# Splitting the last two output blocks of a recurrent attention step into column halves

## The chip, the core and the metric

The kernel runs on one core of one Trainium2 chip. The core has five engines that work side by side and meet through semaphores: TensorE (matrix products, PE in the profile; its weight loads are listed as PEld), VectorE (DVE), ScalarE (ACT), GpSimd (POOL) and SyncE (SP), which here only issues transfers. Matrix products are summed in PSUM, a small memory of eight banks; VectorE and ScalarE copy results out of it. Everything else lies in SBUF, and weights that do not fit there come from the chip's main memory again in every step, by DMA. The metric is the device time of one execution in microseconds (us). Before the change it is 1872.4 us, the median of three runs (1871.83 to 1874.24).

## What is computed

The reference has two parts that share nothing but the output array. Part B is a long convolution with a state-space kernel; the change does not touch it. Part A is attention over 64 segments of 32 rows, one after the other, with a memory of 8 rows that each segment passes on to the next:

```
for s in range(n_seg):                      # 64 segments
    xs = x[:, s * seg_len:(s + 1) * seg_len, :]
    h = concatenate([mem, xs], axis=1)      # 8 + 32 rows, 1024 wide
    q, k, v = h @ Wq, h @ Wk, h @ Wv        # 32 heads of 128
    p = softmax(where(mask, q k^T * scale, -1e9))
    o = (p v) @ Wo                          # back to 1024 columns
    mem = o[:, :8, :]                       # the state of the next segment
    outs.append(o[:, 8:, :])
```

So the output projection of one segment must be finished, at least for the memory rows, before the key, query and value projections of the next can begin.

## The kernel before

Part B runs first, together with all work of part A that does not depend on the memory: the projections of the last 8 rows of each segment are made ahead for all segments and stored in main memory (PKd holds their keys and queries, VXd their values and the other 24 rows of the input, transposed). Then comes a loop over 64 steps, one per segment (`part_a`, from line 408). After the loop a last stage makes the output rows that were left over.

In a step the stationary operand of a projection is `hT`, the transposed input: 32 columns (24 rows of the segment and the 8 memory rows) for each of eight blocks of 128 features, the "key blocks" kc 0 to 7. Since 32 columns fill a quarter of TensorE's array, four matmuls of 512 columns run side by side in four column strips (`quads`, line 409). A block of weights is 128 x 2048. Most blocks stay in SBUF all the time; 13 per step are streamed from main memory through five slots (`stage`, line 340, issued by SyncE; a slot's next load waits until its last reader is done). Three blocks live elsewhere: key block 7 of the first key projection, half of query block 7, and half of output block 15. They are kept in PSUM as raw words, and in every step VectorE copies them into a work area in SBUF just ahead of their use (`fetch`, line 364, through `words`, line 337). Key block 7 comes in five pieces, K7a to K7d and one in a small tile `S_`; the half of output block 15 comes in three, Oa, Ob and again `S_`.

The work area (`arena`) is one tile in which many short-lived tiles share places, by the table `AT` of line 37: "pk", the keys and queries made ahead for the next step, lies at place 0.

The order of the work is the order in which the program is written: each engine runs its own instructions strictly in that order (`manual_schedule`), and waits are derived from which places are read and written. A step has this order: key projection of the first 16 heads (k0), query projection (q0), then the same for the second 16 heads, values, and between them transposes, scores, softmax (VectorE and ScalarE) and the products with the values. Then the output projection `oproj` (line 522) adds 16 blocks into one PSUM tile `pp[:, 1, :]`: four strips of 32 rows, each strip 256 of the 1024 output columns, so a block has eight matmuls of 256 columns. Blocks 0 to 7 take the first 16 heads, and the order of the others is 8, 10, 12, 14, 9, 11, 13, 15; block 13 is streamed, block 15 is the half-fetched one.

What follows is the boundary between two steps (lines 624 to 643). The sums are copied to SBUF as `osb` in two halves of 128 columns, the first by VectorE and the second by ScalarE (line 627); TensorE makes a small product for the left-over rows (`pl`, line 629), transposes both halves (line 633), and VectorE copies the eight memory rows of each transposed half into `hT` (line 635). The first half holds the even key blocks and the second the odd ones; k0 takes the blocks in the order 0, 2, 4, 6, 1, 3, 5, 7. Behind the second of these copies VectorE fetches key block 7 (line 637). ScalarE issues the load of the next "pk" (line 640) and the store of the step's results (line 643) on its own queue; GpSimd later copies parts of "pk" beside the keys (line 430), and the scores (line 441) need them.

Of the kernel before, what the change touches and what calls it, by code (L numbers as in the profile page):

```python
# [10 lines left out]
BF16 = mybir.dt.bfloat16  # L11
F32 = mybir.dt.float32
I32 = mybir.dt.int32
I16 = mybir.dt.int16
ALU = mybir.AluOpType
# [21 lines left out]
AT = {"K7a": 3072, "K7b": 1024, "K7c": 2048, "K7d": 4192, "ob": 4960, "pk": 0, "vx": 3392, "Q7a": 2048, "Q7b": 3072,  # L37
# [3 lines left out]


def weight_blocks(Wq, Wk, Wv, Wo):
# [221 lines left out]
def load_resident(tc, pool, src, key, W_res, eng=None, t_=None):  # L265
    if t_ is None:
        t_ = pool.tile([128, 2048], BF16, name="W_%s" % "_".join(str(i) for i in key))
    (eng or tc.nc.sync).dma_start(out=t_[:].rearrange("e (h d) -> e h d", h=2) if key[0] == "o" else t_[:], in_=src(key))
    W_res[key] = t_


def part_a(ctx, tc, x, src, WD, HE, seg_len, out_a, ahead, W_res, rest, places, first):
    nc = tc.nc
    S, Dm = x.shape
    M = 8
    SL = seg_len
    E = 128
    KC = Dm // 128
    NS = S // SL
    assert SL == 32 and M == 8 and Dm == 1024 and HE == 4096  # L280
    XM = 24
# [5 lines left out]
    ident, mask, BD, BDx, BDL, hT = ahead.consts  # L287
# [14 lines left out]
    def unit(key):  # L302
        if key in rest:

            rest.remove(key)
            load_resident(tc, wres, src, key, W_res, None, outs.pop(0) if outs else places.pop(0)() if places else None)
        if key in W_res:
            return W_res[key]
        if key in KEPT:
            return ahead_of.pop(key) + halves.get(key, [])  # L310
        between.pop(key, lambda: None)()
        if key in first:
            return first.pop(key)
        t_ = stage(key, WD[key][:])
        if key[0] == "v":
            for k_ in rest[0:3 if key[1] == 0 else 1]:
                rest.remove(k_)
                load_resident(tc, wres, src, k_, W_res, None, outs.pop(0) if outs else places.pop(0)() if places else None)
        return t_
# [3 lines left out]
    ps = ctx_l.enter_context(tc.tile_pool(name="a_ps", bufs=1, space=PSUM))  # L323
# [4 lines left out]
    def at(name, *dims):  # L328

        n = int(np.prod(dims))  # L330
        t_ = arena[:, AT[name] // 2:AT[name] // 2 + n]
        if len(dims) == 1:
            return t_
        names = "abc"[:len(dims)]
        return t_.rearrange("p (%s) -> p %s" % (" ".join(names), " ".join(names)), **dict(zip(names, dims)))
# [28 lines left out]
    def fetch(key):  # L364

        ahead_of[key] = []
        for name, lo, n in KEPT[key]:
            t_ = at(name, n) if name else S_[:, 0:n]
            words(t_, kept[key][lo // 1024][:, lo % 1024 // 2:(lo % 1024 + n) // 2])
            ahead_of[key].append((lo, n, t_))  # L370

    def columns(w, lo, n):

        if not isinstance(w, list):
            return [(0, w[:, lo:lo + n])]
        return [(max(lo, l_) - lo, t_[:, max(lo, l_) - l_:min(lo + n, l_ + n_) - l_]) for l_, n_, t_ in w if l_ < lo + n and lo < l_ + n_]
# [31 lines left out]
    for s in range(NS):  # L408
        def quads(m, t, kcs, a=None):
            if a is None:  # L410
                a = ps.tile([128, 512], F32, name="acc", tag=BANK[m, t])
            for kc in kcs:
                w = unit((m, t, kc))
                for g in range(4):
                    for o_, rhs in columns(w, 512 * g, 512):
                        nc.tensor.matmul(a[32 * g:32 * g + 32, o_:o_ + rhs.shape[1]], lhsT=hT[:, kc, :], rhs=rhs,  # L416
                                         start=(kc == 0), stop=(kc == KC - 1), tile_position=(0, 32 * g), skip_group_check=True)
            return a

        def evac(a, name):  # L420
            q = at(name, 512)
            nc.scalar.copy(out=q, in_=a[:])  # L422
            return q
# [95 lines left out]

            pv(pl, t, V, L[:, 0].rearrange("p (a b) k -> p a (b k)", a=4), [L[:, 1].rearrange("p a k -> p (a k)")])  # L520

        def oproj(po, us, oT):
            for u in us:
                w = unit(("o", u))
                for hh in range(2):
                    h = 2 * u + hh
                    for qt in range(4):
                        for o_, rhs in columns(w, 1024 * hh + 256 * qt, 256):
                            nc.tensor.matmul(po[32 * qt:32 * qt + 32, o_:o_ + rhs.shape[1]], lhsT=oT[:, h % 4, (h % 16) // 4, :], rhs=rhs,  # L529
                                             start=False, stop=(h == 31), tile_position=(0, 32 * qt), skip_group_check=True)  # L530

        a = quads("k", 0, (0, 2, 4, 6, 1, 3, 5, 7))
        k0 = evac(a, "k0")
        if s == 0:
            for key in (("q", 0, 7), ("k", 0, 7), ("o", 15)):
                load_kept(key)
        a = quads("q", 0, range(0, 6))
# [5 lines left out]
        a = quads("k", 1, range(0, 3))  # L543
# [16 lines left out]
        a = quads("q", 1, range(KC))  # L560
# [3 lines left out]
        a = quads("v", 0, range(0, 4))  # L564
# [34 lines left out]
        a = quads("v", 1, range(0, 5))  # L599
        vl = vx[:, 0:256].rearrange("p (t e) -> p t e", t=2)  # L600
        pv0 = pv_x(0, V0, pb0, lb0)
        pp = ps.tile([128, 2, 256], F32, name="pp", tag="b3")
# [5 lines left out]
        lb1 = at("lb1", 512)  # L608
# [9 lines left out]
        o1 = evac_o(pv1, "o1", 2)  # L618
        lt1 = turn(weigh(sc1, 1, "ln1"), "lt1")
        oproj(pp[:, 1, :], range(5, 8), o0)  # L620
        L1 = left_blocks(lt1, 0, "L1")
        fetch(("o", 15))
        oproj(pp[:, 1, :], (8, 10, 12, 14, 9, 11, 13, 15), o1)
        ob = at("ob", 2, 256)
        osb = ob[:, 0, :]
        for j in range(2):
            (nc.scalar.copy if j else nc.vector.tensor_copy)(out=osb[:, 128 * j:128 * j + 128], in_=pp[:, 1, 128 * j:128 * j + 128])  # L627
        pl = ps.tile([128, 4, 32], F32, name="pl", tag="b2")
        pv_l(pl[:], 1, V1, L1)
        if s + 1 < NS:  # L630
            pt_o = [ps.tile([128, 4, SL], BF16, name="tro", tag=tag) for tag in ("b0", "b1")]
            for j in range(2):
                nc.tensor.transpose(out=pt_o[j][:].rearrange("p a b -> p (a b)"), in_=osb[:, 128 * j:128 * j + 128], identity=ident[:])
            for j in range(2):
                nc.vector.tensor_copy(out=hT[:, :, XM:SL].rearrange("p (q j) r -> p j q r", j=2)[:, j], in_=pt_o[j][:, :, XM:SL])
        if s + 1 < NS:
            fetch(("k", 0, 7))
        nc.scalar.copy(out=ob[:, 1, 0:128], in_=pp[:, 0, 0:128])
        if s + 1 < NS:
            pk = load_pk(s + 1)  # L640
        nc.scalar.copy(out=ob[:, 1, 128:256], in_=pl[:].rearrange("p a k -> p (a k)"))
        if s + 1 < NS:
            stores(s, ob)

    order = sorted(range(16), key=lambda u: ("o", u) not in W_res)
# [18 lines left out]
    for b in range(4):  # L664
        pe = [ps_k.tile([128, 512], F32, name="pe", tag="keep%d" % (2 * (b % 2) + n)) for n in range(2)]
        for u in order:
            for hh in range(2):
                h = 2 * u + hh
                hi = 16 * (h // 16) + 4 * (h % 4) + (h % 16) // 4
                for n in range(2):  # L670
                    nc.tensor.matmul(pe[n][:], lhsT=left[2 * b + hi // 16][:, 128 * (hi % 16):128 * (hi % 16) + 128],  # L671
                                     rhs=wo[u][:, 1024 * hh + 512 * n:1024 * hh + 512 * n + 512], start=(u == order[0] and hh == 0),
                                     stop=(u == order[-1] and hh == 1))
# [1129 lines left out]
```

## Time and profile before

| | |
|---|---|
| median of three runs | 1872.4 us (1871.83 to 1874.24) |
| profiled execution, its own time | 1879.37 us |
| span of its profile | 1877.7 us |
| granted TensorE clock, mean | 0.98 |
| TensorE busy | 1766.8 us (94%) |
| VectorE busy | 1344.5 us (72%) |
| ScalarE busy | 925.1 us (49%) |
| moved by DMA | 627.78 MB, mean 334 GB/s |

The profile is one execution, recorded by hardware. Its rows name the line of the kernel, the engine, the operation, what is written and read (`out<-in`), the shapes and, behind "x", how many instructions are merged in the row. In a timeline the first two numbers are the start and the duration in us from the start of the span; the bracket at the end is the idle time of the engine before, and who ended it. A row of waits gives the waiting engine, line and tile, then whom it waited for, the total in us, how often, and the longest. In a row by stretch each engine's busy time and instruction count follow the length of the stretch, and the last three numbers are the granted clock, the busy share of the DMA engines and GB/s. "issue" means that the profile names nothing that was waited for. TensorE's matmuls overlap in its pipeline, so starts say more than ends: four matmuls of 512 columns in four strips start again every 0.21 us or so, though each is listed with nearly 0.4 us.

### The profile page before, as it was taken

To read this page: it belongs to the slowest core of one execution; us is meant where nothing else is said; L and a number is where in the kernel's file an instruction comes from. 1 tells how busy PE (TensorE), PEld (TensorE's weight loads), DVE (VectorE), ACT (ScalarE), POOL (GpSimd) and SP (SyncE) were. 2 spreads that over 40 slices of the span, in tenths; PEclk is the share of its full clock that TensorE was granted. 3 is DMA by queue.
4 is the path that set the end of the run, shared out by engine and by line. 5 is a ranking of instruction groups with operands and counts; after the bars stand their busy time and mean duration, and the time that the engine had idled before them with its cause. 6 is when DMAs were issued, how large, how long until landed. Compare 5 with 4: busy or idle time off the path is not lost.

```text
span 1877.7 us, 73879 instructions
## 1 busy us (share of the span) xinstructions
PE 1766.8 (94%) x31563; PEld 1084.5 (58%) x31563; DVE 1344.5 (72%) x3365; ACT 925.1 (49%) x1663; POOL 523.9 (28%) x908
## 2 busy tenths in 40 slices
PE   8999999877987999999999999999999999999999
PEld 3666665546764555555555555555555555555554
DVE  8599989889992666676667676766667666767650
ACT  8799999871112344444344444444444444444420
POOL 2355454437872121111112121211111111111130
PEclk8999999889997999999999999999999999999999
DMA  7889899678899999999999999999999999999992
GB/s 224 238 247 276 262 268 267 191 207 290 262 320 348 391 377 377 391 381 391 375 375 388 365 384 385 378 387 381 367 395 384 373 377 378 377 383 386 383 366 78
DMA packets 350962, 627.78 MB, mean 334 GB/s; under 512 B 95125, under 2 KB 217501, under 8 KB 348585
## 3 DMA queue, kind: packets, MB, share of 16 engines
q1 hardware_dynamic: 307160, 568.55, 85.1%
q10 hardware_dynamic: 36816, 29.59, 4.8%
q0 software_dynamic: 6656, 24.92, 3.6%
q8 instruction: 247, 4.05, 0.9%
q14 instruction: 83, 0.67, 0.1%
HBM read 565.48 MB, written 72.16 MB: 340 GB/s over the span
## 4 chain that ended last, share of the span: by engine, by line
PE 60%; DMA 16%; DVE 13%; ACT 6%; issue 3%; POOL 1%; SPq 0%; DVEq 0%; POOLq 0%; ACTq 0%
PE acc L416 28%; PE pp L529 13%; DMA wst<-WD_v 5%; PE pe L671 3%; DMA arena<-VXd 3%; PE tr L427 3%; DMA wq<-Ud 2%; PE pv L497 2%; DMA wst<-WD_q 2%; DMA wst<-WD_o 2%; PE pv L501 2%; DVE nr L1280 1%; PE pro L184 1%; PE pro L197 1%; ACT sn L1285 1%
## 5 line engine op out<-in xcount | busy, mean ns | idle before, releaser
L416 PEld LDWEIGHTS <-a_hT 128*32 128x32 bf16 x12351 | 324.1, 96 | 292.5 <-issue 39.2
L422 ACT CAST arena<-acc 128x512 bf16<-128x512 f32 x384 | 224.8, 585 | 374.5 <-PE acc L416 311.4
L416 PE MATMUL acc<-wst,a_hT 128*32 128x512 bf16 x2560 | 256.2, 382 | 16.9 <-DMA wst<-WD_v 10.3
L529 PEld LDWEIGHTS <-arena 128*32 128x32 bf16 x8256 | 216.4, 97 | 69.5 <-issue 43.7
L430 POOL COPY arena<-arena 128x128 bf16<-128x128 bf16 x128 | 37.4, 292 | 671.3 <-PE tr L427 383.0
L338 DVE TENSOR_SCALAR arena<-keep 128x256 int32<-128x256 int32 x506 | 173.5, 395 | 25.2 <-PE acc L416 25.2
L416 PE MATMUL acc<-XM,a_hT 128*32 128x512 bf16 x2560 | 185.9, 383 | 0.0
L197 PE MATMUL pro<-XM,wsl 128*128 128x512 bf16 x512 | 124.4, 387 | 3.5 <-DVE XM L112 2.0
L456 DVE TENSOR_REDUCE a_mx<-sc 128x4 f32<-128x160 f32 (+1 forms) x192 | 71.7, 373 | 71.2 <-PE sc L444 69.8
L529 PE MATMUL pp<-W_o,arena 128*32 128x256 bf16 x3072 | 120.2, 274 | 2.1 <-issue 1.9
L416 PE MATMUL acc<-W,a_hT 128*32 128x512 bf16 x1286 | 119.5, 386 | 0.1
L460 ACT ACTIVATE sc<-sc 128x160 f32<-128x160 f32 (+1 forms) x192 | 63.9, 333 | 113.1 <-DVE sc L457 112.9
L548 DVE COPY arena<-tr 128x512 bf16<-128x512 bf16 x64 | 27.2, 425 | 123.0 <-PE tr L427 121.5
L464 DVE TENSOR_REDUCE a_mx<-sc 128x4 f32<-128x160 f32 (+1 forms) x192 | 72.8, 379 | 55.6 <-ACT sc L460 55.3
L491 POOL TENSOR_TENSOR arena<-arena,a_BD 128x128 bf16<-128x128 bf16 x128 | 51.0, 399 | 211.6 <-DVE arena L474 203.4
L416 PE MATMUL acc<-W_q,a_hT 128*32 128x512 bf16 x1536 | 108.1, 379 | 0.0
L529 PE MATMUL pp<-W,arena 128*32 128x256 bf16 x2560 | 105.5, 274 | 1.8 <-issue 1.8
L1280 DVE TENSOR_SCALAR nr<-ptt 128x456 f32<-128x456 int16 x128 | 80.2, 627 | 29.5 <-PE ptt L1258 26.5
L1272 ACT ACTIVATE E<-pa 128x648 bf16<-128x648 f32 x128 | 87.8, 711 | 15.9 <-PE pa L1264 14.1
L627 ACT CAST arena<-pp 128x128 bf16<-128x128 f32 x64 | 17.0, 265 | 151.9 <-DVE arena L627 151.9
L416 PE MATMUL acc<-wq,a_hT 128*32 128x512 bf16 x1024 | 90.5, 382 | 0.0
L416 PE MATMUL acc<-g,a_hT 128*32 128x512 bf16 x1024 | 90.2, 382 | 0.0
(343 smaller groups left out, 3980.9 us busy)
## 6 DMA issues: line engine op xcount, KB each, us to landing
wst<-WD_k SPq DMA_DIRECT2D x256, 512.0 KB
wst<-WD_v SPq DMA_DIRECT2D x256, 512.0 KB
wst<-WD_o SPq DMA_DIRECT2D x192, 512.0 KB
wst<-WD_q SPq DMA_DIRECT2D x128, 512.0 KB
Ud<-ux POOLq DMA_DIRECT2D x16, 1024.0 KB, 8.6
wq<-Ud SPq DMA_DIRECT2D x32, 512.0 KB
wsl<-in_A_Wk_dram SPq DMA_DIRECT2D x16, 512.0 KB
wsl<-in_A_Wv_dram SPq DMA_DIRECT2D x16, 512.0 KB
```

The source lines that it names most:

```text
L197: nc.tensor.matmul(a[:], lhsT=w[:, kc, 128 * j:128 * j + 128], rhs=xTl[:, kc, :, :].rearrange("p s k -> p (s k)"), start=(kc == 0), stop=( ...
L338: nc.vector.tensor_scalar(out=out.bitcast(I32), in0=in_.bitcast(I32), scalar1=0, scalar2=None, op0=ALU.bitwise_or)
L416: nc.tensor.matmul(a[32 * g:32 * g + 32, o_:o_ + rhs.shape[1]], lhsT=hT[:, kc, :], rhs=rhs, start=(kc == 0), stop=(kc == KC - 1), tile_pos ...
L422: nc.scalar.copy(out=q, in_=a[:])
L427: nc.tensor.transpose(out=p[:, hl, :, :].rearrange("p a b -> p (a b)"), in_=q[:, 128 * hl:128 * hl + 128], identity=ident[:])
L456: nc.vector.tensor_reduce(out=m_, in_=x, axis=AX.X, op=ALU.max)
L460: nc.scalar.activation(out=flat(sc, i), in_=flat(sc, i), func=ACT.Exp, scale=scale)
L464: nc.vector.tensor_reduce(out=m_, in_=x, axis=AX.X, op=ALU.add)
L529: nc.tensor.matmul(po[32 * qt:32 * qt + 32, o_:o_ + rhs.shape[1]], lhsT=oT[:, h % 4, (h % 16) // 4, :], rhs=rhs, start=False, stop=(h == 3 ...
L671: nc.tensor.matmul(pe[n][:], lhsT=left[2 * b + hi // 16][:, 128 * (hi % 16):128 * (hi % 16) + 128], rhs=wo[u][:, 1024 * hh + 512 * n:1024 ...
L1272: sc.activation(out=T["E", r, e // 4][:, lo:lo + 8 * NE].rearrange("p (i c) -> p i c", i=2), in_=T.pop(("p", r, e))[:, :, 0:4 * NE], func= ...
L1280: v.tensor_scalar(out=T["n", r, e // 4][:, lo:lo + 8 * NT], in0=T.pop(("t", r, e))[:, 0:8 * NT].bitcast(I16)[:, 0:16 * NT:2], scalar1=floa ...
```

## The change

The last two output blocks, 13 and 15, are no longer added as whole 256-column matmuls. First all of their columns 0 to 127 are added into `pp[:, 1, 0:128]`, then all of their columns 128 to 255 into a new PSUM tile `po` in another bank, which starts from zero.

ScalarE copies the finished first half to `osb`, and then the sums that the other 14 blocks had left in the second half to a new f32 tile `pj` at place 0 of the work area. The first half is transposed right away, ahead of the small product `pl`, and VectorE copies its memory rows into `hT`. VectorE then adds `po` and `pj` into the second half of `osb`.

The second half's transpose moves into the next step, behind key blocks 0 and 2 of its k0 projection (`turned`): there TensorE transposes it, VectorE copies its memory rows into `hT`, and then fetches key block 7. The load of the next "pk" is issued behind both copies of the left-over results, and its place overlaps that of `pj`. The PSUM banks of the small tiles are renamed accordingly.

```
+        def state(j, pt):
+            nc.vector.tensor_copy(out=hT[:, :, XM:SL].rearrange("p (q j) r -> p j q r", j=2)[:, j], in_=pt[:, :, XM:SL])
+
+        def turned(osb):
+            pt_o = ps.tile([128, 4, SL], BF16, name="tro", tag="b2")
+            nc.tensor.transpose(out=pt_o[:].rearrange("p a b -> p (a b)"), in_=osb[:, 128:256], identity=ident[:])
+            state(1, pt_o)
+            fetch(("k", 0, 7))
...
-        def oproj(po, us, oT):
+        def oproj(po, us, oT, lo=0, opens=None):
             for u in us:
-                w = unit(("o", u))
+                w = us[u] if isinstance(us, dict) else unit(("o", u))
                 for hh in range(2):
                     h = 2 * u + hh
                     for qt in range(4):
-                        for o_, rhs in columns(w, 1024 * hh + 256 * qt, 256):
+                        for o_, rhs in columns(w, 1024 * hh + 256 * qt + lo, po.shape[1]):
                             nc.tensor.matmul(po[32 * qt:32 * qt + 32, o_:o_ + rhs.shape[1]], lhsT=oT[:, h % 4, (h % 16) // 4, :], rhs=rhs,
-                                             start=False, stop=(h == 31), tile_position=(0, 32 * qt), skip_group_check=True)
-
-        a = quads("k", 0, (0, 2, 4, 6, 1, 3, 5, 7))
+                                             start=(h == opens), stop=(h == 31), tile_position=(0, 32 * qt), skip_group_check=True)
+
+        a = quads("k", 0, (0, 2))
+        if s > 0:
+            turned(osb)
+        quads("k", 0, (4, 6, 1, 3, 5, 7), a)
         k0 = evac(a, "k0")
...
-        oproj(pp[:, 1, :], (8, 10, 12, 14, 9, 11, 13, 15), o1)
+        oproj(pp[:, 1, :], (8, 10, 12, 14, 9, 11), o1)
+        ends = {u: unit(("o", u)) for u in (13, 15)}
+        po = ps.tile([128, 128], F32, name="po", tag="b2")
+        oproj(pp[:, 1, 0:128], ends, o1)
+        oproj(po[:], ends, o1, 128, 26)
         ob = at("ob", 2, 256)
-        osb = ob[:, 0, :]
-        for j in range(2):
-            (nc.scalar.copy if j else nc.vector.tensor_copy)(out=osb[:, 128 * j:128 * j + 128], in_=pp[:, 1, 128 * j:128 * j + 128])
-        pl = ps.tile([128, 4, 32], F32, name="pl", tag="b2")
+        osb, pj = ob[:, 0, :], at("pj", 256).bitcast(F32)
+        nc.scalar.copy(out=osb[:, 0:128], in_=pp[:, 1, 0:128])
+        nc.scalar.copy(out=pj, in_=pp[:, 1, 128:256])
+        if s + 1 < NS:
+            pt_o = ps.tile([128, 4, SL], BF16, name="tro", tag="b0")
+            nc.tensor.transpose(out=pt_o[:].rearrange("p a b -> p (a b)"), in_=osb[:, 0:128], identity=ident[:])
+        pl = ps.tile([128, 4, 32], F32, name="pl", tag="b1")
         pv_l(pl[:], 1, V1, L1)
         if s + 1 < NS:
-            pt_o = [ps.tile([128, 4, SL], BF16, name="tro", tag=tag) for tag in ("b0", "b1")]
-            for j in range(2):
-                nc.tensor.transpose(out=pt_o[j][:].rearrange("p a b -> p (a b)"), in_=osb[:, 128 * j:128 * j + 128], identity=ident[:])
-            for j in range(2):
-                nc.vector.tensor_copy(out=hT[:, :, XM:SL].rearrange("p (q j) r -> p j q r", j=2)[:, j], in_=pt_o[j][:, :, XM:SL])
-        if s + 1 < NS:
-            fetch(("k", 0, 7))
+            state(0, pt_o)
+        nc.vector.tensor_tensor(out=osb[:, 128:256], in0=po[:], in1=pj, op=ALU.add)
         nc.scalar.copy(out=ob[:, 1, 0:128], in_=pp[:, 0, 0:128])
+        nc.scalar.copy(out=ob[:, 1, 128:256], in_=pl[:].rearrange("p a k -> p (a k)"))
         if s + 1 < NS:
             pk = load_pk(s + 1)
-        nc.scalar.copy(out=ob[:, 1, 128:256], in_=pl[:].rearrange("p a k -> p (a k)"))
-        if s + 1 < NS:
             stores(s, ob)
```

In the table of places the entry `"pj": 0` is added.

2 rows, old and new, of the table AT are left out of this document.

## The prediction

> **What bounds the kernel now.** I read the page first, then the timeline of one step boundary, then the waits, then busy time and transfers by stretch. The page gives the span, the engines' shares and the chain of work that ended last:
>
> ```profile
> span 1877.7 us, 73879 instructions
> PE 1766.8 (94%) x31563; PEld 1084.5 (58%) x31563; DVE 1344.5 (72%) x3365; ACT 925.1 (49%) x1663; POOL 523.9 (28%) x908
> PE 60%; DMA 16%; DVE 13%; ACT 6%; issue 3%; POOL 1%; SPq 0%; DVEq 0%; POOLq 0%; ACTq 0%
> ```
>
> TensorE leads, transfers come second. The 64-step loop fills the span from about 579 to 1818 us. Its period comes from the state transposes: two per boundary, 63 boundaries (first row, view by line). Two timeline rows of neighbouring boundaries give a quick step:
>
> ```profile
> L633 PE MATMUL tro<-a_ident,arena x126: 216/229/230, 615.3 to 1795.3; 128*128 128x128 bf16 x126
> ...
> 995.00 0.53 PE L633 MATMUL tro<-a_ident,arena 128*128 128x128 bf16 x2
> ...
> 1013.55 0.53 PE L633 MATMUL tro<-a_ident,arena 128*128 128x128 bf16 x2
> ```
>
> The last start is a second transpose, 0.3 us behind its first, so 62 steps take 1795.0 - 615.3 = 1179.7 us: 19.03 us each, while this quick one takes 18.55. So a step has 18.55 us of TensorE's own order, boundary gap included, and on average 0.48 us (30 us over the loop) of stalls that come and go. The waits inside those steps and the transfers by stretch say what they are:
>
> ```profile
> PE pp L529 <- issue: 7.8, 12, 1.6
> PE pv L501 <- DMA arena<-VXd: 3.1, 7, 0.6
> PE acc L416 <- DMA wst<-WD_q: 2.5, 4, 0.9
> PE acc L416 <- DMA wst<-WD_v: 2.3, 8, 0.5
> ...
> PE pp L529 <- DMA wst<-WD_o: 1.1, 2, 0.7
> ...
> 615.30:1795.00 1179.70, 1146.73 (x24862) 679.67 (x24862) 806.63 (x2542) 507.89 (x1117) 209.85 (x496) 1.00 1.00 381
> ...
> 1206.00:1208.00 2.00, 2.00 (x41) 1.04 (x37) 1.62 (x7) 0.10 (x2) 0.00 (x0) 1.00 0.97 324
> 1208.00:1210.00 2.00, 2.00 (x40) 1.02 (x32) 0.61 (x2) 0.92 (x2) 0.00 (x0) 1.00 0.87 312
> ```
>
> In the long row the last three numbers are the granted clock (1.00), the DMA share (1.00) and 381 GB/s: the DMA engines are never free for long, with a dip only just after a boundary (0.97 and 0.87). Transfers are nearly a second bound, yet TensorE waits little for them by name (2.5 + 2.3 + 1.1 us for streamed weights). Now the boundary itself:
>
> ```profile
> 1184.67 0.65 DVE L338 TENSOR_SCALAR arena<-keep 128x256 int32<-128x256 int32 x2
> 1184.79 0.39 PE L529 MATMUL pp<-wst,arena 128*32 128x256 bf16 x8
> ...
> 1185.24 0.21 DVE L338 TENSOR_SCALAR a_S<-keep 128x64 int32<-128x64 int32 x1
> 1185.37 0.11 PEld L529 LDWEIGHTS <-arena 128*32 128x32 bf16 x2 [0.17 <-issue]
> 1185.51 0.22 PE L529 MATMUL pp<-a_S,arena 128*32 128x128 bf16 x1
> ...
> 1185.76 0.29 DVE L627 CAST arena<-pp 128x128 bf16<-128x128 f32 x1 [0.31 <-PE pp L529]
> ...
> 1186.08 0.27 ACT L627 CAST arena<-pp 128x128 bf16<-128x128 f32 x1 [2.27 <-DVE arena L627]
> ...
> 1186.11 0.53 PE L633 MATMUL tro<-a_ident,arena 128*128 128x128 bf16 x2
> 1186.15 0.33 ACTq L380 DMA_DIRECT2D arena<-PKd  x1
> ...
> 1186.37 0.47 DVE L635 COPY a_hT<-tro 128x32 bf16<-128x32 bf16 x2 [0.32 <-PE tro L633]
> 1186.40 0.10 PEld L633 LDWEIGHTS <-arena 128*128 128x128 bf16 x1 [0.20 <-ACT arena L627]
> ...
> 1186.61 0.40 PE L416 MATMUL acc<-Wlow,a_hT 128*32 128x512 bf16 x4
> 1186.76 1.34 DVE L338 TENSOR_SCALAR arena<-keep 128x256 int32<-128x256 int32 x4
> ...
> 1188.02 0.21 DVE L338 TENSOR_SCALAR a_S<-keep 128x64 int32<-128x64 int32 x1
> ...
> 1188.13 0.39 PE L416 MATMUL acc<-arena,a_hT 128*32 128x512 bf16 x4
> 1188.32 0.22 PE L416 MATMUL acc<-a_S,a_hT 128*32 128x128 bf16 x1
> 1188.34 0.62 PE L416 MATMUL acc<-W_q,a_hT 128*32 128x512 bf16 x8
> ```
>
> Two chains are visible. The short one goes from the last output matmul (1185.51) over two copies one behind the other, and two transposes, to the next step's first key matmul (1186.61). The long one is VectorE's: behind the second state copy it fetches key block 7 out of PSUM in five pieces, 1186.76 to 1188.23 (1.47 us), and the last piece arrives 0.09 us before the matmul that needs it (1188.32). That second chain has no slack.
>
> **The change, costed on this step.**
>
> *First half earlier.* Blocks 13 and 15 now run columns 0 to 127 first. The piece of block 15 in "Ob" lands at 1185.32 (1184.67 + 0.65) and is needed by this half; the "a_S" piece (1185.45) only by the second. So the first half's last matmul starts at 1185.37, not a full half sooner: 0.14 ahead of today's last. Matmul start to copy start is 0.25 (1185.51 to 1185.76), so ScalarE copies 1185.63 to 1185.90 (0.27). The transpose starts 0.05 later, 1185.95; 0.26 from transpose to state copy (1186.11 to 1186.37): 1186.21; half of 0.47 for one copy, and 0.06 to TensorE: first key matmul at 1186.45. Gain: 0.16 us a step. The wait of ScalarE for VectorE's copy goes with it.
>
> *Second half.* Sixteen matmuls of 128 columns run behind it in another bank. In all these two blocks go from 17 matmuls to 32 with the same columns. Blocks of 8 by 256 columns follow each other by 0.22 (1184.79 on), 0.027 each; half of that is 0.013, so 16 take 0.21 and end near 1185.61. At most they take 0.027 each, 0.43, to 1185.83; both ends lie before the transpose at 1185.95, so I take the columns' price and charge nothing. That cover is 0.1 us at the worse end. The chain of waits bounds the price from below with a smaller form:
>
> ```profile
> 1173.89 0.09 PE sc L441 x16
> ```
>
> Sixteen matmuls of 40 columns in 0.09 us, 0.006 each. The Trainium skill, "TensorE: Matmul & The Clock Gate", Part 1, "Wait — 56ns, not 53.3ns?", says the opposite of such halving: start to start never falls below about 25 ns however few the columns. By that the first half would take an estimated 0.40 instead of 0.21 us; in this step the wait for "Ob" would still hide it, and where it did not, the sum would be up to 0.19 x 63 = 12 us higher. The score matmuls here, four strips wide, run four times below that floor, so I do not use it.
>
> *Sum on VectorE.* ScalarE's second copy, 0.27 (range 0.27 to twice that for the wider output), ends by 1186.17 to 1186.44. The cast (0.29) goes; an add comes, for which no row stands: nearest are 0.29 (this cast, same size) and twice that as the dear end. I take 0.33. It starts behind the state copy, at 1186.39, and ends at 1186.72 (dear end 1186.97).
>
> *Second transpose.* It stands behind two key blocks: 1186.45 + 0.43 (1186.61 to 1187.05 for two) = 1186.88. The add is covered by 0.16 less the 0.05 to TensorE; the dear end would cost 0.14. The state copy then runs 1187.14 to 1187.32; key blocks 4 and 6 end at 1187.37 behind the transpose, so the odd blocks start on time.
>
> *The fetch of key block 7.* This is the cost. It is queued on VectorE behind that state copy; today it starts 0.08 before the copy ends, so 1187.24, and takes 1.47: last piece at 1188.71, its matmul at 1188.80, block q0 at 1188.81 against 1188.34 today. TensorE itself would reach that piece near 1188.2, so it waits about 0.6, and loses **0.47 us net a step** with the 0.16 gain already in. Over 63 boundaries: +29.6 us. Bounds: 0.43 if the add is cheap and the records' spacing is generous, 0.61 with the dear add: 27 to 38 us.
>
> *The next key and query rows.* Their load leaves ScalarE's queue at 1186.15 today. Its destination now holds the second copy, so it waits for the add, about 1186.7: 0.55 later. Queued behind it is only the result store. Who waits for it:
>
> ```profile
> POOL arena L430 <- DMA arena<-PKd: 256.2, 41, 12.4
> ...
> 1192.10 0.29 POOL L430 COPY arena<-arena 128x128 bf16<-128x128 bf16 x1 [6.52 <-DMA arena<-PKd]
> 1192.44 0.17 PEld L441 LDWEIGHTS <-arena 128*32 128x32 bf16 x15 [0.22 <-issue]
> ```
>
> In 41 places GpSimd's copy waits for this load, and in this step the scores start right behind it. Since TensorE comes 0.47 later too, the load is only 0.08 later against it: 0 to 41 x 0.08 = 3 us, say 1. SyncE's queue gains no instruction; streamed weights are asked for as their slots are freed, the first 0.16 earlier, those behind block 7 0.47 later. GpSimd has nothing moved.
>
> *What the stalls give back.* A step with 0.47 us more of TensorE's time leaves the transfers that much more. At least the named weight waits, 6 us, should shrink away; at most all 30 us of stalls. Waits put down to "issue" at matmuls of an already begun block are not for weights and remain. I take 12, nearer the named rows.
>
> **Sum:** 29.6 + 1 - 12 = +18.6, rounded to +18 us. The profiled execution took 1879.4 us, so 1897 there. The median of the runs shown is 1872.4, 7 us lower; the same difference on it gives **1890 us**.
>
> **Rivals.**
> 1. *Nothing is absorbed.* The stalls are latencies, not a lack of transfer time, and stay: 29.6 + 3, so 1905. For it: the small weight waits by name. Against: the DMA share of 1.00.
> 2. *All is absorbed.* If 19.03 us is the transfers' pace and 18.55 only TensorE's, a TensorE order of 19.02 (18.55 + 0.47) fits just under it: 1872, no change. For it: that share, and 381 GB/s. Against: the quick steps at 18.55 show transfers keeping up.
> 3. *Faster.* The first slot is freed 0.16 earlier, just where the transfers dip (0.87); if they set the pace everywhere, each step shortens by that while block 7's wait falls where weights would have been awaited: 63 x 0.16 = 10, so 1862. It decides only if the late fetch costs under 0.16 net of what weights cost at that place; but the matmuls just behind block 7 (W_q, last row of the boundary) use resident weights and wait for no load.
> 4. *The first half is not earlier at all* (its copy waits for the whole output): the 0.16 is lost too, 63 x 0.63 = 40, less 12: 1900.
>
> **Chances.** The forecast 0.60, nothing absorbed 0.18, all absorbed 0.10, faster 0.08, no earlier half 0.04. Slower by over 0.2% (3.7 us, about what a measurement of this kernel can tell from none) is 0.82, same 0.10, faster 0.08. The forecast's own range is 1878 to 1900. The 8-in-10 range reaches to the unabsorbed case and down to near no change: 1874 to 1906.
>
> **What would show it.** In the changed profile the first key matmul should stand about 0.94 us behind the start of today's last output matmul's place (1.10 now), the second transpose behind eight key matmuls, and the five fetch pieces should begin about 0.5 us after the add ends and end 0.09 us before the last piece of block 7 is multiplied, with TensorE idle for 0.5 us or so before it. Quick steps should take near 19.02 us. Weight waits should shrink. I am wrong if the fetch is not what TensorE waits for, if VectorE's add takes over 0.6 us, or if the mean step stays at 19.03 because transfers paced it.

## The result, and the profile after

The changed kernel takes 1922.25 us, the median of five runs (1919.45 to 1926.87), beside 1874.24 us for the kernel before on the same chip: slower by about 48 us by the medians, and by a ratio of 1.0245 (95% interval 1.0212 to 1.0279), which makes 46 us. The forecast was 1890 us with a range of 1874 to 1906: the direction was right, the size was not.

The page of the changed kernel, and its transfers of instructions:

```profile
span 1918.6 us, 76003 instructions
PE 1796.2 (94%) x32472; PEld 1109.5 (58%) x32523; DVE 1338.8 (70%) x3365; ACT 936.8 (49%) x1727; POOL 519.9 (27%) x908
...
q8 instruction: 255, 4.18, 0.9%
...
PE 64%; DVE 13%; DMA 11%; ACT 5%; issue 4%; POOL 2%; SPq 1%; DVEq 0%; POOLq 0%; ACTq 0%
```

The span grew by 40.9 us, and in the chain "issue", time for which the profile names no cause, went from 3% to 4% while the transfers' share fell from 16% to 11%. The boundary of a quick step, by the timeline:

```profile
632.96 0.65 DVE L338 TENSOR_SCALAR arena<-keep 128x256 int32<-128x256 int32 x2
633.09 0.28 PE L538 MATMUL pp<-wst,arena 128*32 128x128 bf16 x8
633.20 0.23 PE L538 MATMUL pp<-Whalf,arena 128*32 128x128 bf16 x4
...
633.93 0.27 ACT L642 CAST arena<-pp 128x128 bf16<-128x128 f32 x1 [1.83 <-PE pp L538]
...
634.25 0.23 PE L646 MATMUL tro<-a_ident,arena 128*128 128x128 bf16 x1
...
634.61 0.28 DVE L651 TENSOR_TENSOR arena<-po,arena 128x128 bf16<-128x128 f32 x1
...
634.75 0.40 PE L416 MATMUL acc<-Wlow,a_hT 128*32 128x512 bf16 x4
634.97 0.33 ACTq L380 DMA_DIRECT2D arena<-PKd  x1
...
635.29 0.23 PE L425 MATMUL tro<-a_ident,arena 128*128 128x128 bf16 x1
...
635.45 0.40 PE L416 MATMUL acc<-Wlow,a_hT 128*32 128x512 bf16 x4
635.56 0.18 DVE L421 COPY a_hT<-tro 128x32 bf16<-128x32 bf16 x1 [0.67 <-PE tro L425]
635.65 1.34 DVE L338 TENSOR_SCALAR arena<-keep 128x256 int32<-128x256 int32 x4
...
636.91 0.21 DVE L338 TENSOR_SCALAR a_S<-keep 128x64 int32<-128x64 int32 x1
637.05 2.25 PEld L416 LDWEIGHTS <-a_hT 128*32 128x32 bf16 x45 [0.17 <-issue]
637.18 0.40 PE L416 MATMUL acc<-W_q,a_hT 128*32 128x512 bf16 x3
637.21 0.22 PE L416 MATMUL acc<-a_S,a_hT 128*32 128x128 bf16 x1
```

Counted from the first row (the fetch of output block 15), the first key matmul stands at 1.79 us (1.94 before) and the query projection at 4.22 (3.67 before): the boundary's gain is there, and the late fetch of key block 7 takes it back and 0.55 more.

### The profile page after: what moved, and what is told of

Its sections match the earlier page's. It is cut to its first block, busy times and chain, and to the rows that moved or that the text cites. A ratio compares the mean times of both kernels' runs of the same rounds, so it can differ in the third digit from the quotient of the medians.

```text
span 1918.6 us, 76003 instructions
## 1 busy us (share of the span) xinstructions
PE 1796.2 (94%) x32472; PEld 1109.5 (58%) x32523; DVE 1338.8 (70%) x3365; ACT 936.8 (49%) x1727; POOL 519.9 (27%) x908
## 3 DMA queue, kind: packets, MB, share of 16 engines
q8 instruction: 255, 4.18, 0.9%
## 4 chain that ended last, share of the span: by engine, by line
PE 64%; DVE 13%; DMA 11%; ACT 5%; issue 4%; POOL 2%; SPq 1%; DVEq 0%; POOLq 0%; ACTq 0%
PE acc L416 32%; PE pp L538 12%; DMA wst<-WD_v 4%; PE tr L436 3%; PE pe L684 3%; DMA wst<-WD_o 2%; PE pv L506 2%; DVE nr L1293 2%; DMA arena<-PKd 2%; PE pv L510 2%; PE pro L197 1%; PE pro L184 1%; DMA wq<-Ud 1%; PE ptt L1271 1%; DVE gr L1259 1%
## 5 line engine op out<-in xcount | busy, mean ns | idle before, releaser
L416 PEld LDWEIGHTS <-a_hT 128*32 128x32 bf16 x12351 | 346.1, 96 | 289.1 <-issue 64.1
L416 PE MATMUL acc<-wst,a_hT 128*32 128x512 bf16 x2560 | 263.6, 382 | 17.5 <-DMA wst<-WD_v 9.8
L538 PEld LDWEIGHTS <-arena 128*32 128x32 bf16 x9216 | 222.4, 96 | 77.9 <-issue 48.4
L197 PE MATMUL pro<-XM,wsl 128*128 128x512 bf16 x480 | 119.4, 387 | 4.8 <-DVE kst L206 1.5
L416 PE MATMUL acc<-W_q,a_hT 128*32 128x512 bf16 x1536 | 113.3, 383 | 0.0
L421 DVE COPY a_hT<-tro 128x32 bf16<-128x32 bf16 x126 | 22.0, 175 | 103.1 <-PE tro L646 56.2
```

Of the source, the lines that this page charges most:

```text
L197: nc.tensor.matmul(a[:], lhsT=w[:, kc, 128 * j:128 * j + 128], rhs=xTl[:, kc, :, :].rearrange("p s k -> p (s k)"), start=(kc == 0), stop=( ...
```

## The experiments

Two numbers per kernel are compared. The *mean step* comes from the small product `pl`, which each of the 64 steps makes once: its last start less its first, by 63. The *quick step* is the shortest distance between two of them in the trace, what the engines need when nothing comes late. It is firm where many steps share it to 0.01 us (before, changed, `e2`, `e5`, `e8`, `e10` to `e12`; four steps in `e4`). Elsewhere it is less so, since a product that itself starts late makes the step behind it look short: the next shortest are 18.94 in `e1`, 18.80 in `e3` (shared by nine), 18.50 in `e6`, 20.34 in `e7`, 18.55 in `e9` and 18.93 in `e13`. The `pl` rows by tile (first and last start) for the kernels that the argument rests on are these, in the order before, changed, `e2`, `e9`, `e10`, `e11`, `e12`:

```profile
L497 PE MATMUL pl<-arena x256: 176/176/190, 614.8 to 1817.6; 128*128 128x32 bf16 x128
```
```profile
L506 PE MATMUL pl<-arena x256: 176/177/209, 615.2 to 1858.4; 128*128 128x32 bf16 x128
```
```profile
L503 PE MATMUL pl<-arena x256: 176/176/190, 618.9 to 1845.2; 128*128 128x32 bf16 x128
```
```profile
L497 PE MATMUL pl<-arena x256: 176/176/190, 619.7 to 1845.4; 128*128 128x32 bf16 x128
```
```profile
L497 PE MATMUL pl<-arena x256: 176/176/190, 608.2 to 1780.2; 128*128 128x32 bf16 x128
```
```profile
L497 PE MATMUL pl<-arena x256: 176/176/190, 617.7 to 1789.9; 128*128 128x32 bf16 x128
```
```profile
L506 PE MATMUL pl<-arena x256: 176/177/189, 618.7 to 1828.9; 128*128 128x32 bf16 x128
```

For the kernel before that is (1817.6 - 614.8) / 63 = 19.09 us. Times are medians, each beside the kernel before on its own chip; the ratio carries the interval. The steps are those of one traced execution, which in `e8` took 1905.01 us and in `e9` 1907.26, 14 and 10 above their medians.

| kernel | time, us | before, us | ratio (95%) | quick step | mean step |
|---|---|---|---|---|---|
| before | | | | 18.55 | 19.09 |
| changed | 1922.25 | 1874.24 | 1.0245 (1.0212 to 1.0279) | 19.15 | 19.73 |
| e1 two pieces ahead | 1925.09 | 1878.06 | 1.0240 (1.0202 to 1.0278) | 18.78 | 19.80 |
| e2 moved alone | 1904.43 | 1878.06 | 1.0133 (1.0100 to 1.0167) | 19.30 | 19.47 |
| e3 extra transpose | 1887.32 | 1878.06 | 1.0036 (1.0017 to 1.0055) | 18.59 | 19.14 |
| e4 halves, not moved | 1917.26 | 1878.06 | 1.0186 (1.0142 to 1.0230) | 18.81 | 19.64 |
| e5 rows early | 1919.17 | 1879.92 | 1.0211 (1.0185 to 1.0238) | 19.15 | 19.68 |
| e6 sum on first half | 1915.06 | 1876.81 | 1.0195 (1.0159 to 1.0230) | 18.49 | 19.59 |
| e7 all in halves | 2149.18 | 1876.81 | 1.1415 (1.1369 to 1.1461) | 19.98 | 23.27 |
| e8 key blocks cut | 1890.82 | 1876.81 | 1.0074 (1.0048 to 1.0099) | 18.58 | 19.42 |
| e9 two blocks cut | 1897.52 | 1876.81 | 1.0106 (1.0072 to 1.0139) | 18.49 | 19.46 |
| e10 before, half loads | 1844.20 | 1879.92 | 0.9816 (0.9785 to 0.9847) | 18.54 | 18.60 |
| e11 cut, half loads | 1850.69 | 1879.92 | 0.9842 (0.9810 to 0.9874) | 18.54 | 18.61 |
| e12 changed, half loads | 1888.12 | 1879.92 | 1.0043 (1.0024 to 1.0061) | 19.15 | 19.21 |
| e13 all halves, half loads | 1961.14 | 1878.35 | 1.0456 (1.0429 to 1.0483) | 18.88 | 20.35 |

### Is it the late fetch?

The theory of the prediction: key block 7 comes late on VectorE. Its rival: something else in the change. `e1` fetches two of the five pieces where VectorE idles:

```
         nc.vector.tensor_tensor(out=osb[:, 128:256], in0=po[:], in1=pj, op=ALU.add)
+        if s + 1 < NS:
+            fetch(("k", 0, 7), 0, 2)
...
             state(1, pt_o)
-            fetch(("k", 0, 7))
+            fetch(("k", 0, 7), 2)
```

> The changed kernel, with two of the five pieces of key block 7 fetched by VectorE behind the add, ahead of the second state copy, where VectorE is idle today (0.67 us). Late fetch: the last piece comes 0.67 us sooner, TensorE no longer waits for it, and the step loses 0.57 - 0.12 = 0.45 us: 1922 - 28 = about 1894. If the second transpose between the key blocks cost TensorE nothing itself: 1886. If the halves, the late row load or the longer instruction stream are the cause: unchanged, about 1922.

The wait went, and the time stayed. A boundary of `e1`, by the timeline:

```profile
673.03 0.75 DVE L338 TENSOR_SCALAR arena<-keep 128x256 int32<-128x256 int32 x2
...
674.47 0.21 DVE L338 TENSOR_SCALAR a_S<-keep 128x64 int32<-128x64 int32 x1
...
674.77 0.39 PE L417 MATMUL acc<-arena,a_hT 128*32 128x512 bf16 x4
674.94 0.22 PE L417 MATMUL acc<-a_S,a_hT 128*32 128x128 bf16 x1
674.98 0.61 PE L417 MATMUL acc<-W_q,a_hT 128*32 128x512 bf16 x8
```

The last piece is there 0.26 us ahead of its matmul, and the quick step fell from 19.15 to 18.78 (the next shortest is 18.94), at most 0.37 of the 0.45 expected; but the mean step is 19.80. So the late fetch as the only cause falls: with it gone, other stalls fill its place. The waits between 620 and 1790 us name one of them, first of the changed kernel, then of `e1`:

```profile
PE sc L450 <- POOL arena L439: 3.2, 6, 1.3
POOL arena L439 <- DMA arena<-PKd: 163.9, 24, 8.5
```
```profile
PE sc L451 <- POOL arena L440: 19.0, 32, 1.6
POOL arena L440 <- DMA arena<-PKd: 308.4, 43, 8.5
```

In `e1` the scores wait 19.0 us, in 32 places, for GpSimd's copy of the rows loaded for the step, and GpSimd waits for that load. In the changed kernel TensorE comes to the scores later, and waits there for 3.2 us. So the 0.37 us gained at the fetch (23 us over 63 steps) is for the most part lost again at the scores. `e1` with the row load of `e5` was not run.

`e2` does only the move (the second transpose, its state copy and the fetch, behind two key blocks), in the kernel before:

```
-        a = quads("k", 0, (0, 2, 4, 6, 1, 3, 5, 7))
+        a = quads("k", 0, (0, 2))
+        if s > 0:
+            turned(osb)       # transpose of osb[:, 128:256], state copy, fetch(("k", 0, 7))
+        quads("k", 0, (4, 6, 1, 3, 5, 7), a)
```

> The kernel before, with only the second half's transpose, its state copy and the fetch of key block 7 moved behind the next step's first two key blocks: no column halves, no add, row load as before. Late fetch: the last piece is multiplied about 0.74 us later than before, 63 x 0.74 = 47 us: about 1921. If the halves, the add or the row load are the cause: 1874 to 1880.

Its quick step is 19.30, 0.75 over before, as worked out; but the time grew by 26 us, not 47, since the mean step grew by only 0.38. Its stalls have nearly vanished: mean less quick is 0.17 us, where the kernel before has 0.54.

`e4` is the other part: halves, add and late row load, with the second transpose, its state copy and the fetch put back to the end of the step (edit of the changed kernel):

```
         a = quads("k", 0, (0, 2))
-        if s > 0:
-            turned(osb)
...
         nc.vector.tensor_tensor(out=osb[:, 128:256], in0=po[:], in1=pj, op=ALU.add)
+        if s + 1 < NS:
+            turned(osb)
```

> The changed kernel, with the second transpose, its state copy and the fetch of key block 7 back at the end of the step, behind the add: column halves, add and late row load stay. Late fetch: the fetch starts about 0.35 us sooner than in the changed kernel, its last piece is multiplied about 0.25 us later than in the kernel before: 16 us, with the late row load up to 12 more, 1890 to 1902. If halves, add or row load are the cause: about 1922.

It is 39 us slower, far above the 16 to 28 expected. By the trace 63 x 0.26 = 16 us of that lie in the quick step, as worked out, and the stalls grow from 0.54 to 0.83 us a step. So what stays in `e4` (halves, add and late row load) costs time by itself, in stalls.

`e3` prices a lone transpose between key blocks, added to the kernel before:

```
+        if s > 0:
+            extra = ps.tile([128, 4, SL], BF16, name="trx", tag="b1")
+            nc.tensor.transpose(out=extra[:].rearrange("p a b -> p (a b)"), in_=osb[:, 128:256], identity=ident[:])
```

> The kernel before, plus one transpose per step between the second and third key block that nobody reads. If a lone transpose between key blocks costs TensorE 0.06 us, as predicted: 1874 to 1878. If it costs 0.27 us (the rows of the changed kernel: 0.54 us from the first key block to it where two blocks take 0.43, and 0.16 behind it): 63 x 0.24 = 15 us, about 1889.

It cost 9 us by the medians, between the two, and 7 by the ratio of 1.0036. Of this the loop has only 3 us in the trace (63 x 0.05, the mean step); the rest arose ahead of it, where `pl` begins at 620.0 us and not at 614.8. The price at the place is the dear one: in `e3` as in the changed kernel the transpose starts 0.55 us (median) behind the first key matmul, where two key blocks take 0.43, and the next matmul 0.16 behind it. The 18.80 us that nine of its steps share have it, 0.25 over before. Most of it comes back: the mean step is only 0.34 above that, where the kernel before has 0.54.

### The halves: instructions, not columns

What is new in the halves beside columns is the number of instructions: 32 matmuls and weight loads in place of 17. The profile's queue q8 carries what looks like TensorE's instruction stream: 4.05 MB in 247 transfers before, and 2 x 31563 matmuls and weight loads make 64 bytes each of that; it is 4.18 MB in the changed kernel and 5.10 MB where all blocks are cut. New theory: TensorE uses up instructions faster than they come. `e9` cuts the matmuls of blocks 13 and 15 and changes nothing else; `e8` cuts four key blocks, where a matmul takes longer; `e7` cuts all output blocks.

```
# e9 (e7: cut = 128 for every u)
-                        for o_, rhs in columns(w, 1024 * hh + 256 * qt, 256):
+                        cut = 128 if u in (13, 15) else 256
+                        for o_, rhs in [(n + o_, r) for n in range(0, 256, cut) for o_, r in columns(w, 1024 * hh + 256 * qt + n, cut)]:
# e8, in quads
-                    for o_, rhs in columns(w, 512 * g, 512):
+                    for o_, rhs in [(n + o_, r) for n in range(0, 512, cut) for o_, r in columns(w, 512 * g + n, cut)]:
                     # cut = 256 for key blocks 3 to 6 of the second key projection, else 512
```

> The kernel before, with each 256-column matmul of output blocks 13 and 15 cut in two of 128 columns one behind the other, in the same bank and order: 17 matmuls become 32 a step, nothing else changes. New theory, instruction supply: TensorE uses up its instructions faster than they are brought in, so the quickest step stays at 18.55 us but stalls in the middle of output blocks grow by 0.2 to 0.35 us a step: 12 to 22 us slower than before. If the cut matmuls are harmless: within 3 us of before.

> The kernel before, with four key blocks of the second key projection cut from 512 to 256 columns per matmul: 16 more matmuls a step, as many as in the changed kernel, but in a stretch where a matmul takes longer. Instruction supply by rate: within 4 us of before. Instruction supply by the mere number: 12 to 22 us slower, as with the two output blocks. Neither: within 3 us.

> The kernel before, with every output block in matmuls of 128 columns: about 127 more matmuls a step, same columns. Instruction supply: a step's output projection (256 matmuls and as many weight loads) takes 3.4 us by columns but stalls by 1 us or more: 60 us or more slower. A floor of 25 ns per matmul: 256 x 25 = 6.4 us in place of 3.4, 190 us slower. Harmless: within 5 us of before.

The cut of two blocks alone costs 21 us, with the quick step where it was; the four key blocks cost 14, so the mere number counts, also in a slower stretch (whether it costs less there is not settled: the two intervals overlap); all blocks cost 272. The waits of TensorE's matmuls between 620 and 1790 us, first of the kernel before, then `e9`, then `e7`:

```profile
PE pp L529 <- issue: 7.8, 12, 1.6
...
PE acc L416 <- issue: 1.2, 3, 0.5
```
```profile
PE pp L530 <- issue: 12.7, 18, 2.2
PE acc L416 <- issue: 9.1, 13, 1.6
```
```profile
PE pp L529 <- issue: 158.0, 76, 4.4
...
PE acc L416 <- issue: 4.4, 5, 2.1
```

"issue" is what grows. Take the places where a matmul starts over 0.5 us after the one before it although both belong to one group (same line, output and operands), and set them beside the records of single packets. The changed kernel has 21 in the loop, and each ends 1.2 to 1.7 us after an instruction packet of q8 has landed, though there are only 205 such packets in 63 steps, one in 6 us.

The places themselves say more. A packet of q8 has 16384 bytes, which is 256 instructions of 64. Number TensorE's records in order, two for each matmul with its weight load and one for each of its three semaphore records a step, and divide by 256: in the kernel before all 11 stops leave the same remainder to within one, in the changed kernel all 21, in `e9` all 32, in `e7` all 95 (over all fifteen traces 366 of 367, the exception in `e6`). So a stop comes only at every 256th instruction, a packet's worth, shortly after a packet has landed: TensorE has used up one packet and waits for the next. From start to start these stops last 10.9 us in the kernel before, 4.1 in `e2`, 20.4 in the changed kernel, 25.8 in `e4`, 32.1 in `e9`, 27.7 in `e8` and 206.8 in `e7`. So the 21 us of `e9` are found in them (32.1 less 10.9).

One such stop, in the middle of the small product (timeline of the changed kernel):

```profile
1381.00 0.23 PE L506 MATMUL pl<-arena 128*128 128x32 bf16 x3
1383.53 0.21 PE L506 MATMUL pl<-arena 128*128 128x32 bf16 x1 [2.30 <-issue]
```

The fourth matmul of that group needs no data that the first three did not have in kind; by its place in the stream it stands on that step of 256.

### Why the instructions are late

If they queue behind the weights, lighter transfers cure it. Half loads:

```
-        nc.sync.dma_start(out=t_[:].rearrange(...) if len(in_.shape) == 3 else t_[:], in_=in_)
-        return t_
+        nc.sync.dma_start(out=t_[:, 0:1024], in_=in_[:, 0:1024])
+        return [(0, 1024, t_[:, 0:1024]), (1024, 1024, t_[:, 0:1024])]
```

> The kernel before, with only the first half of each block that is streamed in the loop loaded, and its two halves of columns multiplied from the same 1024 columns: same instructions, 13 loads a step of half the size; the output is not the reference's. If the stalls of the loop come from crowded transfers, weights and instructions alike, nearly all steps take 18.55 us: 1877 - 30 = about 1847. If the instruction stalls are not from the crowd: about 1857.

> The same half loads (output not the reference's), with the 256-column matmuls of blocks 13 and 15 cut in two as in the run that did only this. If the cut costs time because instructions queue behind the weights in crowded transfers: as the kernel before with half loads, about 1847. If TensorE is limited by the supply whatever the transfers do: about 20 us above that, 1867.

> The changed kernel with the same half loads (output not the reference's). Only the fixed part of the change is left, the late fetch of key block 7: 0.60 us a step more than the kernel before with half loads, 63 x 0.60 = 38 us: about 1885.

The DMA share falls to 0.67 (row by stretch, `e10`, against 1.00 before), and the stalls of all three kernels vanish: mean and quick step agree within 0.07 us.

```profile
620.00:1790.00 1170.00, 1155.92 (x25085) 684.03 (x25078) 814.45 (x2568) 511.67 (x1125) 214.46 (x507) 1.00 0.67 209
```

The cut of two blocks now costs nothing in the loop (18.61 against 18.60); the 6.5 us between `e11` and `e10` arose ahead of it (`pl` begins at 617.7 against 608.2, in stretches where the two kernels are alike; over all traces it begins between 608 and 620). The changed kernel keeps 0.61 us a step, the late fetch: 38 us in the loop, 44 by the times. "DMA: Bandwidth & Descriptors" of the Trainium skill ("Issuing engines are not separate DMA queues") says that transfers started by different engines run on the same 16 DMA engines and interleave; it does not speak of instructions, but the three runs agree with it and show that they share the crowd. How a packet comes late is not shown: once begun it takes as long under full loads (median 1.03 us in the loop of the kernel before) as under half (0.98 in `e10`), so the delay lies ahead of its start, and the trace does not tell when it was asked for.

`e13`, the kernel `e7` with the edit to half loads, asks whether the cut matmuls are also limited by a rate.

> The kernel before with half loads (output not the reference's) and every output block in matmuls of 128 columns. If the 272 us that this cut cost under full loads are instructions that come late in crowded transfers: the kernel before with half loads, 1844, plus at most the few us that the two cut blocks cost there (6.5): 1844 to 1860. If a matmul of 128 columns and its weight load cannot follow each other faster than about 25 ns for long, whatever the transfers do: 128 x 2 x (25 - 13.3) ns x 64 = 190 us above, about 2035.

Neither end: 117 us above `e10`. The timeline of `e13` shows the matmuls at full pace, then a stop:

```profile
1001.25 0.63 PE L529 MATMUL pp<-W_o,arena 128*32 128x128 bf16 x32
1001.70 0.41 PE L529 MATMUL pp<-W,arena 128*32 128x128 bf16 x16
1001.92 0.28 PE L529 MATMUL pp<-wst,arena 128*32 128x128 bf16 x2
1004.15 0.35 PE L529 MATMUL pp<-wst,arena 128*32 128x128 bf16 x11 [1.95 <-issue]
```

32 matmuls in 0.45 us are 0.014 each, no floor of 25 ns. But with 256 pairs in a row stops of 1.5 us (median) remain even in thin transfers: that many instructions are not held ready. All 64 stops of over 0.5 us in this loop stand on the same step of 256, and together they last 94 us, most of the 117. So here too it is the next instructions that are missing.

### The row load, and a better version

`e5` gives `pj` another place and issues the row load between the two copies of the left-over results, as before:

```
-      "lb1": 4960, "ln1": 0, "lt1": 704, "L1": 2048, "o1": 3936, "Oa": 4960, "Ob": 2560, "pj": 0}
+      "lb1": 4960, "ln1": 0, "lt1": 704, "L1": 2048, "o1": 3936, "Oa": 4960, "Ob": 2560, "pj": 2560}
...
         nc.scalar.copy(out=ob[:, 1, 0:128], in_=pp[:, 0, 0:128])
-        nc.scalar.copy(out=ob[:, 1, 128:256], in_=pl[:].rearrange("p a k -> p (a k)"))
         if s + 1 < NS:
             pk = load_pk(s + 1)
+        nc.scalar.copy(out=ob[:, 1, 128:256], in_=pl[:].rearrange("p a k -> p (a k)"))
+        if s + 1 < NS:
             stores(s, ob)
```

> The changed kernel, with the f32 copy of the second half's sums at another place of the work area (2560 instead of 0) and the load of the next step's key and query rows issued between the two copies of the left-over results, as before the change. If the late row load costs what the waits ahead of the scores show (about 4 us more than before): 1918. If it is hidden: 1922. If it is the main cause of the loss: below 1900.

It is 39 us slower than before, where the changed kernel is 48; the intervals of the two ratios overlap, so a few us at most, not settled. It is not the main cause while the fetch is late as well; with the fetch early it counts for more (the scores in `e1`).

`e6` keeps the halves without the late fetch: the first half of blocks 13 and 15 goes to `po`, and `pj` takes the first half's earlier sums while that runs; the second transpose and the fetch stand at the end of the step, as before, and the first piece of key block 7 is fetched ahead of the state copy, the row load issued between the two copies, as before.

```
+        pj = at("pj", 256).bitcast(F32)
+        nc.scalar.copy(out=pj, in_=pp[:, 1, 0:128])
+        oproj(po[:], ends, o1, 0, 26)
+        oproj(pp[:, 1, 128:256], ends, o1, 128)
...
+        nc.vector.tensor_tensor(out=osb[:, 0:128], in0=po[:], in1=pj, op=ALU.add)
+        nc.scalar.copy(out=osb[:, 128:256], in_=pp[:, 1, 128:256])
```

> A version that keeps the halves and moves nothing into the next step: the first half's last blocks go to the other bank, the sums of the 14 earlier blocks are copied early, VectorE's add ends the first half, ScalarE's copy the second; the row load leaves as before; one piece of key block 7 is fetched ahead of the second state copy. Quickest step by the rows: 0.14 us under before, 63 x 0.14 = 9 us faster if stalls stay as before (about 1867). With instruction supply: the stalls of the other kernels with halves, 0.3 to 0.4 us a step more, come back: 10 to 16 us slower than before.

38 us slower than before, not the 10 to 16 expected, though its shortest step (18.49) is 0.06 under that of the kernel before: 1.1 us of stalls a step. Its 32 stops of over 0.5 us in the middle of a group last 32.5 us. No version that beats the kernel before was found.

## Why the prediction was wrong

In the traces the loop grew by (1858.4 - 615.2) - (1817.6 - 614.8) = 40.4 us: 38 by the quick step (63 x 0.60) and 2.5 by stalls. The forecast had 29.6 + 1 for the first and -12 for the second. By the medians it is 48: the traced execution of the kernel before was 5 us above its median, that of the changed kernel 2 below.

*First half earlier.* Right: the first key matmul 1.79 us behind the fetch of block 15, 1.78 by the sum; the wait for "Ob" gated it as worked out. One slip did no harm: half of 0.47 and 0.06 make 0.30, while its 1186.45 stands 0.24 behind 1186.21; 0.23 was measured (634.75, with the state copy at 634.52).

*Second half.* This step failed. "I take the columns' price and charge nothing" holds for the array: eight matmuls of 128 columns take 0.11 us in the rows above, and the quick step does not move in `e9`. But each is also two instructions to be brought in through transfers that are never free, and that has a price of its own, paid between instruction packets: 21 us in `e9`. The prediction counted DMA issues and never the instruction stream, though the "issue" waits at matmuls of a begun block (7.8 us at line 529) were in its rows; it said that they remain, not that more instructions feed them. Its cover, the idle gap ahead of the transpose, covers TensorE's time, not this.

*Sum on VectorE.* Right: 0.28, off the path (the transpose behind the key blocks stands at the same 0.55 in `e3`, which has no add).

*Second transpose.* Undersized: 0.54 behind the first key matmul, not 0.43, and 0.16 instead of 0.06 behind it. The fetch starts 0.12 later for it.

*The fetch of key block 7.* The mechanism held. Priced at 0.47, measured at 0.55 between the two boundaries' rows, 0.60 in the quick steps and 0.61 with thin transfers (`e12` less `e10`): 38 us over 63 steps against 29.6, the top of the stated bounds.

*The next rows.* Priced at 1 us; a few at most in the changed kernel (`e5`; the scores wait 3.2 us there). But the load is the next wait behind the late fetch: 19.0 us in `e1`.

*What the stalls give back.* This step failed together with the second half. As a term of the move it was too small: the move alone gives back 23 us and not 12, 63 x (0.75 - 0.38) in `e2`, and the transpose alone 13, 63 x (0.25 - 0.05) in `e3`. The waits for weights by name shrank as foretold, from 5.9 to 3.2 us. Yet in the changed kernel nothing is left of it: 0.58 us of stalls a step (19.73 less 19.15), as in the kernel before (0.54). The halves make new ones, 63 x (0.58 - 0.17) = 26 us more than in `e2`; 16 of these are stops between packets (20.4 against 4.1 us), and the rest is not assigned. Rival 1, "nothing is absorbed" (1905), came nearest, by luck: its stalls do give time back.

The two parts done alone, 26 us (`e2`) and 21 us (`e9`), add up to the 48 measured. That they add is an observation, and in the traced loops they do not quite (24 and 23 against 40). With the wait removed by itself (`e1`) the time did not fall, largely because the scores then waited for the row load.

## What to carry to other kernels

Where transfers fill the DMA engines, an instruction is not free because its columns are: count matmuls and weight loads of a change as bytes to be fetched, and look for "issue" waits in the middle of a group before cutting matmuls into smaller ones. Take the quick step and the mean step apart: the first shows what an order costs, the second what late arrivals cost, and a wait removed from the first can come back in the second. Before work is moved behind a wait, look at what is queued behind it on the same engine; here a fetch with 0.09 us of slack carried the whole loss of that part.

## What the runs showed of the hardware

That instruction delivery is a bound at all was not expected: 15 more matmuls and their weight loads in some 400 of each a step cost 1% of the time under full transfers and nothing in the loop under half. The floor of about 25 ns per matmul that the prediction set against the trace ("TensorE: Matmul & The Clock Gate" of the Trainium skill, Part 1) does not hold for these column strips: 0.014 us each for 16 in a row in `e13`. And a stop can cost twice. Around one in `e7`, by stretch, the granted clock is the third number from the right:

```profile
1002.00:1004.50 2.50, 0.63 (x45) 0.46 (x33) 2.19 (x9) 0.61 (x2) 0.76 (x2) 1.00 0.99 356
1004.50:1007.50 3.00, 2.94 (x116) 2.94 (x120) 0.00 (x0) 0.00 (x0) 0.00 (x0) 0.54 0.75 258
1007.50:1010.00 2.50, 2.33 (x46) 1.22 (x38) 1.47 (x6) 0.70 (x3) 0.00 (x0) 0.87 0.68 206
```

After 2.5 us in which TensorE was busy for 0.63, it ran the next 3 us at 0.54 of full speed; the mean clock of `e7` is 0.944 where the other kernels have 0.98. So part of the 272 us there is the slower clock behind the stops. In the loop of `e7` the clock stood at half for 184 us in all (3 in the kernel before, 10 in the changed one); an estimate of the most that this can have cost is half of that, 92 us.
